# Sharing out the filling products of an attention pipeline: even fifths in the first fifteen slots

## The chip, the cores and the metric

The kernel runs on one core of one Trainium2 chip. The metric is the device time of one execution in microseconds (us). All numbers of the profile come from one profiled execution; times "at 46.00" are microseconds from the start of its span.

## The reference

One transformer block over 2048 tokens of width 512, in float32:

```
mod = silu(c) @ w_mod  -> sa, ca, ga, sb, cb, gb
h   = layernorm(x) * (1 + ca) + sa
x1  = x + ga * (attention(h) @ wo)
h2  = layernorm(x1) * (1 + cb) + sb
out = x1 + gb * (((h2 @ w_gate) * (h2 @ w_up)) @ w_down)      # F = 1376

attention: 32 heads of 16, in 4 segments of 512 tokens, per segment s and head:
  a_dot = softmax(q k^T / 4 + causal mask) v
  a_mem = (phi(q) M) / (phi(q) z + 1e-6)       # phi(t) = t+1 if t>0 else exp(t)
  o     = sigmoid(beta) * a_mem + (1 - sigmoid(beta)) * a_dot
  M += phi(k)^T v ;  z += sum phi(k)           # after the segment
```

## The kernel before

**Stages.** After a start of about 28 us (weights, the first layernorm, the first projections) comes the attention loop, and from about 500 us on the feed-forward part (lines from 1289 on). The change lies in the attention loop, in its first fifteen slots.

**The attention loop.** Work is cut into 32 units `u`; a unit is four heads of one segment, two units make one of the four head groups `g` of a segment. The loop over `v` from -2 to 32 is a software pipeline, and each `v` has five slots. In a slot stand, in the order in which the code is written:

- `q_half(u, i, 0)`: the products q_i_0 of the unit that is ahead (line 282). TensorE writes logits into PSUM bank `lq0`; VectorE reads them in a masked row-maximum scan (line 39, `CUSTOM_DVE_ANT_0`) that ends in a `DVE_READ_ACCUMULATOR2_ANT` and so frees the bank.
- `fill(share[slot], slot < 4)`: the filling products, see below.
- `q_half(u, i, 1)`: the same for bank `lq1` (q_i_1).
- `k_step(v, slot)`, for v from 0 on: the transposed logits of the unit in work, into the double bank `lk`; ScalarE takes the exponential (line 335, tile `pt`) and GpSimd zeroes the masked triangles (line 341, `AFFINE_SELECT`).

For v from 1 on, slot 1 also has the 32 products of `av_step` (tile `tb`).

**The filling products.** Two generators, `fa` and `fb`, hand out everything else that TensorE has to do meanwhile: the projections of the next head group and segment (vps, kps, qps: bank tiles of 12 products, handed out three at a time), the memory term (mp, mz) and others. Each call of `fill` adds `share * rate` to a credit, and takes pieces until the credit is used up:

```
def fill(share, mem):
    credit[0] += share * rate[0]          # rate[0] is 5.5 in every slot
    if mem:
        credit[0] -= mem_step() or 0.0    # mp: 0.5, mz: 0.9
    while credit[0] > 0:
        ...                               # w = next piece's weight
        credit[0] -= w                    # 0.68 for three products
```

When the twelve products of a projection are through, its pieces for the other engines follow (`a_kq`, line 800): ScalarE copies it (line 820, `qf`), casts it to bfloat16 (824), GpSimd subtracts (825, `qr`), ScalarE casts the rest (828), GpSimd subtracts again (829), and a transfer stores it (830, `qd`). `load(u)` brings stored q and k back as `qst` and `kst`.

**The next segment's layernorm** (`ln`, line 172) is woven into the same stream: VectorE takes statistics (`ast`, `amv`) of four tiles x_0 to x_3, ScalarE takes Ln and Exp (`asd` line 186, `ay` line 188), GpSimd refines the result in five small steps (lines 192, 196 to 199; the last writes `ay`), and VectorE scales x_0 to x_3 by `ay` (`TENSOR_SCALAR`).

**What sets the order.** TensorE's order is that in which the code is written (every product is tied to the one before). VectorE's is too, from this loop on (`vec.eng = CV`, a chain). The orders of ScalarE, GpSimd and of the transfers issued by SyncE are set by a list scheduler when the kernel is built; on the chip each engine keeps the order that it was given.

Of the kernel before, what the change touches and what calls it, by code (L numbers as in the profile page):

```python
# [57 lines left out]
def tile_kernel(ctx, tc, x, wq, wk_, wv, wo, beta, w_gate, w_up, w_down, c, w_mod, out):  # L58
# [58 lines left out]
    def flush():  # L117

        while later:
            later.pop(0)()  # L120

    def rest_of():

        while soon:
            soon.pop(0)()
# [116 lines left out]
    def run(gen):  # L242
        try:
            while True:
                next(gen)
        except StopIteration as e:
            return e.value
# [34 lines left out]
    def q_half(u, i, b):  # L282

        Q, K = qst[u % NB], kst[u % NB]
        if i == b == 0:
            nms[u] = ap.tile([P, 16], F32, tag="nm", name=f"nm{u}", bufs=2)
        nm = nms[u]
        h = i // 2 * 2 + b
        if i == 4:
            parts = ((2 * b, 1), (2 * b + 1, 1))  # L290
        else:
            parts = ((h, 3),) if i % 2 == 0 else ((h, 2), (h, 0))
        qp = psp.tile([P, L], F32, tag=f"lq{b}", name=f"q{u}_{i}_{b}", bufs=1)
        c = 0
        for hh, qb in parts:
            n = (qb + 1) * P
            MM(qp[:, c:c + n], Q[0:96, hh, qb * P:(qb + 1) * P], K[0:96, hh, 0:n], start=True, stop=True)
            c += n
        c = 0
        for hh, qb in parts:  # L300
            n = (qb + 1) * P
            vec.tensor_tensor_reduce(qp[:, c:c + n], qp[:, c:c + n], cmask[:, L - n:], -1.0, -NEG,
                                     ALU.add, ALU.min, nm[:, 4 * hh + qb:4 * hh + qb + 1])
            c += n

    def n_step(u):

        Q = qst[u % NB]
        tp = pst([16, P], "tb", f"ntp{u}")
        TP(tp, nms.pop(u), ident)  # L310
        nt = ap.tile([16, 2, P], BF, tag="nt", name=f"nt{u}", bufs=2)
        vec.tensor_copy(nt[:, 0], tp)
        vec.tensor_sub(nt[:, 1], tp, nt[:, 0])
        for i in range(2):
            lastnt[0] = nc.sync.dma_start(Q[96 + i:97 + i].rearrange("p h (q t) -> p (h q) t", t=P), nt[:, i])
# [29 lines left out]
    def av_step(u, kb):  # L345

        s, g, jq = u // 8, u // 2 % 4, u % 2
        if kb == 0:
            tbs[u] = pst([P, L], "tb", f"tb{u}", F32)
        n = L - kb * P  # L350
        for j in range(HQ):
            p, b = j // 2, j % 2
            hh = g * HG + jq * HQ + j
            if kb == 0:
                rhs, w = ptiles[u, p][:, b, :], sels[u, 1]
            elif kb == 2:
                rhs, w = ptiles[u, 4][:, p, 256 * b:256 * b + 256], sels[u, 4]
            else:
                c = 0 if kb == 1 else 384
                rhs, w = ptiles[u, 2 + p][:, b, c:c + n], sels[u, 3]  # L360
            x = MM(tbs[u][32 * j:32 * j + 32, kb * P:], vt[s % 2][kb][:, hh * VS:hh * VS + 32], rhs,
                   start=kb == 0, stop=kb == 2, tile_position=(0, 32 * j), skip_group_check=True)
            if j == 0:
                tc.add_manual_dep(x.ins, w.ins.name, SYNC, reason="all four heads")
        if kb == 2:
            tsbs[u] = ap.tile([P, L], F32, tag="tsb", name=f"tsb{u}", bufs=2)
            act.activation(tsbs[u], tbs.pop(u), AF.Copy)  # L367
# [140 lines left out]
    def wo_load(s, pool):  # L508
        rw = []
        for t in range(4):  # L510
            a = pool.tile([P, D], F32, tag="orl", name=f"orl{s}_{t}", bufs=4)
            n = D - P if s == NSEG - 1 else D
            pin(nc.sync.dma_start(a[:, 0:n], od[s][t][:, 0:n]))
            rw.append(a)
        return rw

    def wo_op(s, rw, us, gs=range(NG), stop=False):

        for g in gs:
            op = bank(f"op{s}_{g}", small=not stop)  # L520
            for t in range(4):
                a = rw[t][:, g * P:(g + 1) * P]
                if s == NSEG - 1 and g == NG - 1:
                    a = orows[NSEG * NG - 1][:, t].rearrange("p h e -> p (h e)")
                TP(op[:, t * P:(t + 1) * P], a, ident)
            nm = ("k", "q")[g % 2]
            i = s % 2 * 2 + g // 2
            oH = pw.tile([P, L], F32R, tag=f"w{nm}H{i}", name=f"oH{s}_{g}", bufs=1)
            oL = pw.tile([P, L], F32R, tag=f"w{nm}L{i}", name=f"oL{s}_{g}", bufs=1)
            ahead.append(act.activation(oH, op, AF.Copy))  # L530
            us.append((oH, oL))
            if stop:
                yield 0.45
                pin(vec.tensor_sub(oL, op, oH.bitcast(F32)))
            else:
                (soon if (s, g) in ((1, 0), (2, 1)) else later).append(lambda oL=oL, op=op, oH=oH: pin(vec.tensor_sub(oL, op, oH.bitcast(F32))))
                yield 0.45
            if stop and g % 2 == 1:
                yield False

    def xr_load(s, pool, tag="xr"):
        xrs = []
        for t in range(4):
            xr = pool.tile([P, D], F32, tag=tag, name=f"xr{s}_{t}", bufs=4)
            pin(nc.sync.dma_start(xr, x[rows(s, t), :]))
            xrs.append(xr)
        return xrs
# [530 lines left out]
    def fill(share, mem):  # L1078

        credit[0] += share * rate[0]  # L1080
        if mem:
            credit[0] -= mem_step() or 0.0
        while credit[0] > 0:
            for f in (fa, fb):
                try:
                    w = next(f)
                    break
                except StopIteration:
                    w = None
            if w is False:  # L1090
                return
            if w is None:
                credit[0] = min(credit[0], 0.5)
                return
            credit[0] -= w

    def until(*key):
        while key not in done:
            credit[0] -= (mem_step() if len(key) == 3 and memq else next(fa)) or 0.0
# [50 lines left out]
    load(1)  # L1150
    btag[:] = ["ms"]
    vec.eng = CV
    share = (0.25, 0.0, 0.25, 0.25, 0.25)
    for v in range(-2, NQ + 1):
        rate[0] = 5.5
        on, prev = 0 <= v < NQ, 0 <= v - 1 < NQ
        for slot in range(5):
            i = (slot + 3) % 5
            u = v + 2 if i < 3 else v + 1
            if 0 <= u < NQ:  # L1160
                q_half(u, i, 0)
            flush()
            if prev and slot == 1:
                for kb in (0, 1, 3, 2):
                    av_step(v - 1, kb)
            if v == NQ and slot == 0:
                assert B["orl_free"]
                o3 = wo_load(3, wpool)
                xr3 = xr_load(3, B["pb"])
            if v == NQ and slot == 2:  # L1170
                for f in (fa, fb):
                    for _ in f:
                        pass
                btag[:] = ["lq0", "lq1", "ms"]
                us3 = []
                run(wo_op(3, o3, us3, range(NG - 1), True))
                lg1 = lnC(1, wpool, lambda: pc, wpool, "orl", 4, lambda name: dbank(name))
                next(lg1)
            if prev and slot == 4:
                if (v - 1) % 2 == 0 and v > 8:  # L1180
                    until((v - 1) // 8, (v - 1) // 2 % 4, 0)
                t_step(v - 1)
                if (v - 1) % 8 == 7:
                    osegs[0] += 1
            if slot == 2 and prev and (v - 1) % 8 == 7:
                vfree[0] = (v - 1) // 8 + 2
            fill(share[slot], slot < 4)
            rest_of()
            if 0 <= u < NQ:
                q_half(u, i, 1)  # L1190
            if on:
                k_step(v, slot)
            while after:
                after.pop(0)()
            while behind:
                behind.pop(0)()
            if slot == 2 and 0 <= v + 1 < NQ:
                n_step(v + 1)
                if v + 3 < NQ:
                    load(v + 3)  # L1200
            if slot == 1 and 3 <= v + 3 < NQ:
                until((v + 3) // 8, (v + 3) // 2 % 4)
# [95 lines left out]
    def dbank(name):  # L1298
        nd[0] += 1
        return pst((P, 512), ("lq0", "lk0", "lq1", "lk1")[nd[0] % 4], name)  # L1300
# [381 lines left out]
```

## Time and profile before

| | |
|---|---|
| three runs | 853.47, 853.55, 854.69 us; median 853.55 |
| the profiled execution | 854.15 us, span 852.4 us |
| TensorE busy | 835.3 us, 98% |
| VectorE busy | 643.1 us, 75% |
| ScalarE busy | 499.0 us, 59% |
| GpSimd busy | 276.8 us, 32% |
| granted TensorE clock | 1.000 |

In the profile PE is TensorE's products, DVE VectorE, ACT ScalarE, POOL GpSimd, SPq the transfers that SyncE issues. A row of the timeline has start, duration, engine, source line, operation, tiles (output<-input, numbers left out), shapes and a count where several are merged; in brackets stands the idle time of the engine just before the row and who ended it. The end of a product is modelled: products that follow each other overlap in the rows, and the distance of their starts tells how fast they are issued.

### The profile page before, as it was taken

The page shows a single profiled execution, that of the slowest core. Times are in us where ns is not written, and L with a number is a line of the kernel's source. Part 1 is how long each engine was busy: PE and PEld are TensorE (multiplying, and loading weights), DVE is VectorE, ACT ScalarE, POOL GpSimd, SP SyncE. Part 2 cuts the span into 40 slices and gives each one's busy share as a digit, 9 for nine tenths or more (in the row PEclk, how much of TensorE's full clock was granted, in tenths as well). Part 3 has the DMA queues.
Part 4 walks back from the last instruction along what each step waited for, and adds up shares of the span by engine and source line. Part 5 has one row for each costly group of instructions (what it writes and reads, how often), then busy time and mean ns, then how long its engine had stood idle before and what let it go on. Part 6 is the DMA issues. An engine that isn't in the chain of part 4 may idle for free.

```text
span 852.4 us, 14404 instructions
## 1 busy us (share of the span) xinstructions
PE 835.3 (98%) x4972; PEld 597.4 (70%) x4972; DVE 643.1 (75%) x1797; ACT 499.0 (59%) x760; POOL 276.8 (32%) x423
## 2 busy tenths in 40 slices
PE   9989999999999999999999999999999999999998
PEld 6756656666665656666665687888888778888886
DVE  7897768887778967787888359989987855447654
ACT  4758767787676876677545626344435555555330
POOL 2756627566565774675434610000000000000000
PEclk9999999999999999999999999999999999999999
DMA  9645435563545554466675466587650685335102
GB/s 271 155 152 155 121 104 141 158 179 115 143 106 166 144 165 106 122 170 213 195 216 155 145 192 230 189 287 271 253 201 28 234 271 210 121 135 184 43 8 98
DMA packets 83928, 139.57 MB, mean 164 GB/s; under 512 B 12720, under 2 KB 46768, under 8 KB 83856
## 3 DMA queue, kind: packets, MB, share of 16 engines
q1 hardware_dynamic: 83424, 138.51, 52.0%
q8 instruction: 39, 0.64, 0.3%
q14 instruction: 33, 0.27, 0.1%
q10 hardware_dynamic: 432, 0.15, 0.1%
HBM read 89.87 MB, written 48.50 MB: 162 GB/s over the span
## 4 chain that ended last, share of the span: by engine, by line
PE 61%; DVE 5%; ACT 1%; issue 0%; POOL 0%; DVEq 0%
PE acc L1358 14%; PE Xg L1289 7%; PE Xu L1289 6%; PE wops L85 5%; PE tb L85 5%; PE Yu L1289 4%; PE Yg L1289 4%; PE k L85 3%; PE q L85 3%; DVE q L39 2%; PE Zg L1289 1%; PE Zu L1289 1%; PE qps L85 1%; PE vps L85 1%; PE Xx L1289 1%; PE up L85 1%
## 5 line engine op out<-in xcount | busy, mean ns | idle before, releaser
L39 DVE CUSTOM_DVE_ANT_0 q<-q,cmask 128x384 f32<-128x384 f32 (+3 forms) x512 | 248.2, 503 | 71.1 <-PE q L85 63.5
L335 ACT ACTIVATE pt<-k 128x1024 f32<-128x1024 f32 x160 | 164.0, 1025 | 74.2 <-PE k L85 71.4
L341 POOL TENSOR_SCALAR_AFFINE_SELECT pt<-pt 128x256 f32<-128x256 f32 (+1 forms) x224 | 98.0, 452 | 137.2 <-ACT pt L335 136.9
L85 PE MATMUL q<-kst,qst 96*128 96x384 bf16 (+3 forms) x512 | 122.8, 302 | 6.5 <-DVE nm L39 5.1
L85 PE MATMUL k<-qst,kst 98*128 98x384 bf16 (+3 forms) x512 | 96.0, 299 | 1.6 <-ACT pt L335 1.3
L1366 DVE TENSOR_TENSOR xa<-xa,acc 128x512 f32<-128x512 f32 x95 | 64.9, 684 | 39.6 <-PE acc L1358 37.8
L85 PEld LDWEIGHTS <-qst 96*128 96x128 bf16 x512 | 43.9, 98 | 58.4 <-issue 43.6
L85 PE MATMUL tb<-pt,v 128*32 128x512 f32 (+3 forms) x1024 | 75.5, 436 | 0.0
L39 DVE DVE_READ_ACCUMULATOR2_ANT nm<- 128x1 f32 x512 | 71.8, 140 | 0.0
L85 PEld LDWEIGHTS <-kst 98*128 98x128 bf16 x512 | 44.4, 98 | 24.9 <-issue 8.8
L1358 PE MATMUL acc<-dH,mH 128*128 128x512 f32 (+1 forms) x152 | 60.3, 397 | 0.0
L1358 PE MATMUL acc<-dL,mH 128*128 128x512 f32 (+1 forms) x152 | 60.1, 395 | 0.0
L1358 PE MATMUL acc<-dH,mL 128*128 128x512 f32 (+1 forms) x152 | 60.0, 395 | 0.0
L85 PEld LDWEIGHTS tb<-pt,v 128*32 128x32 f32 x1024 | 28.7, 109 | 38.6 <-issue 35.7
L367 ACT ACTIVATE tsb<-tb 128x512 f32<-128x512 f32 x32 | 19.1, 596 | 31.6 <-PE tb L85 31.5
L1358 PEld LDWEIGHTS acc<-dH,mL 128*128 128x128 f32 (+1 forms) x152 | 28.5, 188 | 7.1 <-DVE mL L1309 0.3
L1358 PEld LDWEIGHTS acc<-dL,mH 128*128 128x128 f32 (+1 forms) x152 | 28.6, 188 | 7.0
L1358 PEld LDWEIGHTS acc<-dH,mH 128*128 128x128 f32 (+1 forms) x152 | 28.5, 188 | 6.8
L85 PE MATMUL kps<-ahH,wkH 128*128 128x512 f32 x64 | 29.4, 460 | 0.0
L85 PE MATMUL qps<-ahH,wqH 128*128 128x512 f32 x64 | 28.7, 448 | 0.2 <-DVE oL L39 0.2
L85 PE MATMUL vps<-wvH,ahH 128*128 128x512 f32 x64 | 28.3, 442 | 0.0
L85 PE MATMUL wops<-woH,oH 128*128 128x512 f32 x64 | 28.3, 442 | 0.0
(403 smaller groups left out, 2019.1 us busy)
## 6 DMA issues: line engine op xcount, KB each, us to landing
wm<-in_w_mod_dram SPq DMA_DIRECT2D x24, 256.0 KB, 3.9
kd<-k SPq DMA_DIRECT2D x16, 384.0 KB, 2.5
qd<-q SPq DMA_DIRECT2D x16, 384.0 KB, 3.5
kst<-kd SPq DMA_DIRECT2D x32, 192.0 KB, 3.2
qst<-qd SPq DMA_DIRECT2D x32, 192.0 KB, 3.7
x<-in_x_dram SPq DMA_DIRECT2D x16, 256.0 KB, 4.8
kst<-kd SPq DMA_DIRECT2D x32, 128.0 KB, 3.2
qst<-qd SPq DMA_DIRECT2D x32, 128.0 KB, 3.7
```

The lines of the kernel that those rows point to most:

```text
L39: i = getattr(self.eng, name)(*a, **k)
L85: return pe(nc.tensor.matmul(*a, **k))
L335: ex = act.activation(pt, kp, AF.Exp, scale=0.25)
L341: sels[u, i] = nc.gpsimd.affine_select(w, w, pattern=[[0, w.shape[1]], [1, P]], compare_op=ALU.is_ge, fill=0.0, base=0, channel_multiplier=-1)
L367: act.activation(tsbs[u], tbs.pop(u), AF.Copy)
L1289: pe(nc.tensor.matmul(ps[0:n], a, b[:, k], start=first and c == 0, stop=last and c == 5, skip_group_check=True))
L1358: pe(nc.tensor.matmul(ps, a[0:m, t * P:(t + 1) * P], b[0:m], start=j == 0, stop=j == n - 1))
L1366: vec.tensor_add(xa, xa, ps)
```

## The change

The shares of a slot are chosen anew for every `v`. As long as no unit is through (`prev` is false: v = -2, -1 and 0, fifteen slots), each of the five slots gets a fifth; afterwards the old shares hold. The credit of one `v` is 5.5 in both.

```
-    share = (0.25, 0.0, 0.25, 0.25, 0.25)
     for v in range(-2, NQ + 1):
         rate[0] = 5.5
         on, prev = 0 <= v < NQ, 0 <= v - 1 < NQ
+        share = (0.25, 0.0, 0.25, 0.25, 0.25) if prev else (0.2,) * 5
         for slot in range(5):
             i = (slot + 3) % 5
```

Pieces are taken whole, so most stay in their slot. Three groups of three products move on TensorE. The last three of vps_2 come ahead of the first scan product of unit 0 (q_0_0) instead of behind it. The three of kps_2 that use ahH_2 and ahL_2 come behind q_3_1, q_4_0 and the transposes mp_0 of unit 0 instead of ahead of them. The last three of qps_2 move furthest.

This is TensorE at the end of the second `v` and the start of the third; q_ are scan products of unit 1, k_0 the first transposed logits of unit 0, qps_2 the q projection of head group 2. Before:

```order
L88 MATMUL mp_1_768<-ident,phk_1_539 128x128 x4
L85 MATMUL qps_2_732<-ahH_3_397,wqH_517 128x512
L85 MATMUL qps_2_732<-ahH_3_397,wqL_518 128x512
L85 MATMUL qps_2_732<-ahL_3_398,wqH_517 128x512
L85 LDWEIGHTS qst_187
L85 MATMUL q_3_1_787<-kst_183,qst_187 128x384
L85 LDWEIGHTS qst_187
L85 MATMUL q_3_1_787<-kst_183,qst_187 128x128
L85 LDWEIGHTS kst_182
L85 MATMUL k_0_792<-qst_186,kst_182 128x512
L85 LDWEIGHTS kst_182
L85 MATMUL k_0_792<-qst_186,kst_182 128x512
```

The same place now, from the second product of k_0 on:

```order
L85 MATMUL k_0_780<-qst_186,kst_182 128x512
L85 LDWEIGHTS qst_187
L85 MATMUL q_4_0_786<-kst_183,qst_187 128x256
L85 LDWEIGHTS qst_187
L85 MATMUL q_4_0_786<-kst_183,qst_187 128x256
L85 MATMUL mz_1_791<-v_0_162,pkr_1_773 128x136
L85 MATMUL mz_1_791<-v_1_163,pkr_1_773 128x136
L85 MATMUL mz_1_791<-v_2_164,pkr_1_773 128x136
L85 MATMUL mz_1_791<-v_3_165,pkr_1_773 128x136
L85 MATMUL qps_2_732<-ahH_3_397,wqH_517 128x512
L85 MATMUL qps_2_732<-ahH_3_397,wqL_518 128x512
L85 MATMUL qps_2_732<-ahL_3_398,wqH_517 128x512
```

The last three products of qps_2 stood between mp_1 and q_3_1; now they stand behind mz_1, directly ahead of q_4_1.

What hangs on qps_2 moves with it on the other engines. On GpSimd the place is the stretch from the subtraction of the k projection of group 2 to the layernorm's last step; qr_2 (line 825) and q_0_2 (line 829) belong to qps_2, ayb and aya and ay to the layernorm, pt_0 to pt_3 are the masks of unit 0. Before:

```order
L825 TENSOR_TENSOR qr_2_784<-qf_2_781,q_0_2_783 128x512
L341 AFFINE_SELECT pt_0_795<-pt_0_795 128x2x128
L829 TENSOR_TENSOR q_0_2_783<-qr_2_784,q_0_2_783 128x512
L341 AFFINE_SELECT pt_1_817<-pt_1_817 128x2x128
L196 TENSOR_SCALAR ayb_869<-amv_746 128x4
L341 AFFINE_SELECT pt_2_842<-pt_2_842 128x2x128 x2
L192 TENSOR_TENSOR aya_868<-ay_866 128x4
L197 TENSOR_TENSOR ayb_869<-ayb_869,aya_868 128x4
L198 TENSOR_SCALAR ayb_869<-ayb_869 128x4
L199 TENSOR_TENSOR ay_866<-ay_866,ayb_869 128x4
L341 AFFINE_SELECT pt_3_892<-pt_3_892 128x2x128 x2
```

The same stretch now:

```order
L341 AFFINE_SELECT pt_0_783<-pt_0_783 128x2x128
L341 AFFINE_SELECT pt_1_817<-pt_1_817 128x2x128
L825 TENSOR_TENSOR qr_2_806<-qf_2_803,q_0_2_805 128x512
L196 TENSOR_SCALAR ayb_869<-amv_746 128x4
L341 AFFINE_SELECT pt_2_842<-pt_2_842 128x2x128 x2
L829 TENSOR_TENSOR q_0_2_805<-qr_2_806,q_0_2_805 128x512
L192 TENSOR_TENSOR aya_868<-ay_866 128x4
L197 TENSOR_TENSOR ayb_869<-ayb_869,aya_868 128x4
L341 AFFINE_SELECT pt_3_892<-pt_3_892 128x2x128
L198 TENSOR_SCALAR ayb_869<-ayb_869 128x4
L341 AFFINE_SELECT pt_3_892<-pt_3_892 128x2x128
L199 TENSOR_TENSOR ay_866<-ay_866,ayb_869 128x4
```

The subtraction of line 829 now stands just ahead of the layernorm's aya, and the two masks of pt_3, which followed the layernorm's last step, now stand among its steps. On ScalarE pt_0 now precedes the copy of qps_2, and that projection's casts stand behind pt_1 and behind asd. On VectorE only the statistics of x_2 move: from ahead of q_3_1's scan of unit 1 to behind the mz_1 step, ahead of q_4_1's scan. Among the transfers the store of that q projection moves behind the first piece of the load for unit 3. From v = 1 on all engines have their old order, apart from the k projection of group 3, whose last cast and subtraction go ahead of pt_4's exponential and mask.

More of the change, by code (lines that the diff above doesn't have):

```diff
@@ L1152, in tile_kernel @@
     vec.eng = CV
-    share = (0.25, 0.0, 0.25, 0.25, 0.25)
     for v in range(-2, NQ + 1):
@@ L1156, in tile_kernel @@
         on, prev = 0 <= v < NQ, 0 <= v - 1 < NQ
+        share = (0.25, 0.0, 0.25, 0.25, 0.25) if prev else (0.2,) * 5
         for slot in range(5):
```

## The prediction

> **What bounds the kernel now.** First the page's busy times, then the waits, then stretches around the fifteen slots (they run from about 35 to 67).
>
> ```profile
> PE 835.3 (98%) x4972; PEld 597.4 (70%) x4972; DVE 643.1 (75%) x1797; ACT 499.0 (59%) x760; POOL 276.8 (32%) x423
> PE q L85 <- DVE nm L39: 5.1, 11, 1.0
> DVE x L39 <- POOL ay L199: 0.4, 1, 0.4
> 54.00:57.00 3.00, 1.98 (x15) 1.45 (x14) 2.90 (x13) 2.26 (x4) 2.62 (x4) 1.00 0.43 134
> 67.00:70.00 3.00, 3.00 (x39) 1.60 (x39) 2.86 (x10) 2.41 (x4) 1.52 (x2) 1.00 0.04 10
> ```
>
> PE is busy for 98% of the span, so a microsecond that PE stands still anywhere is a microsecond at the end, unless PE waits less later. Its largest wait is for DVE: a scan product needs its bank freed by the last read of the scan before. The two stretches (length, then PE, PEld, DVE, ACT, POOL, clock, DMA) show two regimes. At 54 to 57 DVE is busy for 2.90 of 3.00 us and PE only for 1.98: the scans pace everything. At 67 to 70 PE is full. So the change is judged by what it does to DVE's chain of scans up to about 67, and after that by how late PE is. DVE waits only once in the kernel for the layernorm's `ay`, for 0.4 us; that wait will matter most.
>
> **The first move** (vps_2 ahead of q_0_0 of unit 0).
>
> ```profile
> 33.57 3.80 DVE L853 SCALAR_TENSOR_TENSOR phk<-phk,rlk 128x512 f32<-128x512 f32 x1 [1.02 <-ACT phk L848]
> 36.81 0.39 PE L85 MATMUL vps<-wvH,ahH 128*128 128x512 f32 x1
> ```
>
> Products start 0.23 apart, so q_0_0 moves to just ahead of 36.81, at about 36.6. DVE is busy with the phk step until 37.37 and a scan can begin 0.43 after its product (the next rows: 43.59 and 44.02), 37.03. Cost nothing, covered by 0.3 us.
>
> **The second move** (three products of kps_2 behind q_3_1, q_4_0 and mp_0).
>
> ```profile
> 43.59 0.61 PE L85 MATMUL q<-kst,qst 96*128 96x384 bf16 x4
> 44.02 0.57 DVE L39 CUSTOM_DVE_ANT_0 q<-q,cmask 128x384 f32<-128x384 f32 x1 [0.31 <-PE q L85]
> 45.09 0.38 PE L85 MATMUL q<-kst,qst 96*128 96x256 bf16 x2 [0.45 <-DVE nm L39]
> 45.81 0.14 DVE L39 DVE_READ_ACCUMULATOR2_ANT nm<- 128x1 f32 x1
> 46.00 0.38 PE L85 MATMUL q<-kst,qst 96*128 96x512 bf16 x1 [0.53 <-DMA qd<-q]
> ```
>
> DVE waited 0.31 us for q_3_1 at 44.02. That product now comes 3 x 0.23 = 0.7 us sooner, and the wait is gone. PE loses nothing: the 0.45 us that it idled ahead of q_4_1 now lie ahead of q_4_0, and the three products fill the later gap. Does the gain survive 46.00? The row blames a transfer, but DVE's read ends at 45.95, 0.05 us earlier, the distance that the other bank waits show (below: 55.01 to 55.06), so I read it as a bank wait that moves along. The three products now also delay q_4_1's release, which may eat the gain. Bounds 0 and -0.31; I take the middle, **-0.15 us**.
>
> **The third move** (three of qps_2 behind k_0, q_4_0, mz_1). PE first.
>
> ```profile
> 54.87 0.14 DVE L39 DVE_READ_ACCUMULATOR2_ANT nm<- 128x1 f32 x1
> 55.06 0.38 PE L85 MATMUL q<-kst,qst 96*128 96x256 bf16 x2 [0.66 <-DVE nm L39]
> 55.28 1.09 PE L85 MATMUL mz<-v,pkr 128*128 128x136 f32 x8
> 56.73 0.38 PE L85 MATMUL q<-kst,qst 96*128 96x256 bf16 x2 [0.36 <-DVE nm L39]
> 56.95 0.59 PE L85 MATMUL k<-qst,kst 98*128 98x512 bf16 x2
> 58.32 0.40 PE L85 MATMUL kps<-ahL,wkH 128*128 128x512 f32 x1
> 58.52 0.14 DVE L39 DVE_READ_ACCUMULATOR2_ANT nm<- 128x1 f32 x1
> 58.71 0.38 PE L85 MATMUL q<-kst,qst 96*128 96x512 bf16 x1
> 84.46 1.09 PE L85 MATMUL mz<-v,pkr 128*128 128x136 f32 x8
> 86.09 0.39 PE L85 MATMUL q<-kst,qst 96*128 96x512 bf16 x1
> ```
>
> q_4_0 stays at 55.06: its bank is freed by the read that ends at 54.87 + 0.14 = 55.01. Then mz and three products take 86.09 - 84.46 = 1.63 us (the same two steps, later in the trace), so q_4_1 starts at 55.28 + 1.63 = 56.91 instead of 56.73: 0.18 late. DVE does not feel it, with its scans queued one behind the other, and PE loses it again at q_0_1: the products end their issue at 58.32 + 0.23 = 58.55, and the bank comes free at 58.66, so q_0_1 stays at 58.71. Cost 0 on PE. The statistics of x_2 change places inside a full DVE stretch; before q_4_1's scan the sum of work is the same: 0.
>
> Now what hangs on qps_2. ACT and POOL:
>
> ```profile
> 54.13 0.63 ACT L824 ACTIVATE q<-qf 128x512 bf16<-128x512 f32 x1
> 55.06 1.15 POOL L825 TENSOR_TENSOR qr<-qf,q 128x512 f32<-128x512 f32 x1
> 56.94 1.16 POOL L829 TENSOR_TENSOR q<-qr,q 128x512 bf16<-128x512 f32 x1 [0.38 <-ACT q L828]
> 57.58 1.03 ACT L335 ACTIVATE pt<-k 128x1024 f32<-128x1024 f32 x1 [0.72 <-PE k L85]
> 61.40 0.20 POOL L192 TENSOR_TENSOR aya<-ay 128x4 f32<-128x4 f32 x1
> 61.95 0.14 DVE L39 DVE_READ_ACCUMULATOR2_ANT nm<- 128x1 f32 x1
> 62.03 1.03 ACT L335 ACTIVATE pt<-k 128x1024 f32<-128x1024 f32 x1 [1.02 <-PE k L85]
> 62.25 0.20 POOL L199 TENSOR_TENSOR ay<-ay,ayb 128x4 f32<-128x4 f32 x1
> 62.48 0.55 DVE L39 TENSOR_SCALAR x<-x,amv,ay 128x512 f32<-128x512 f32 x1 [0.40 <-POOL ay L199]
> 63.13 0.77 POOL L341 TENSOR_SCALAR_AFFINE_SELECT pt<-pt 128x256 f32<-128x256 f32 x2 [0.68 <-ACT pt L335]
> 63.51 0.40 PE L85 MATMUL qps<-ahL,wqH 128*128 128x512 f32 x1
> 63.81 0.14 DVE L39 DVE_READ_ACCUMULATOR2_ANT nm<- 128x1 f32 x1
> 64.01 0.38 PE L85 MATMUL q<-kst,qst 96*128 96x512 bf16 x1
> ```
>
> Before, POOL ran its small steps from 61.40 on, 0.28 apart, wrote `ay` at 62.25, and only then waited for pt_3 (ACT until 63.06, masks from 63.13, two in 0.77, so 0.39 each). Now the masks stand among the small steps. From 63.13: mask 0.39, step 198 0.28, mask 0.39, so `ay` starts at 64.19, ends 0.20 later, and DVE's scaling of x_0 starts 0.03 behind that (62.45 to 62.48): **64.42 instead of 62.48, 1.94 late**.
>
> The second path to the same step is the moved subtraction. k_1 starts at 57.13, its exponential 0.63 later (56.95 to 57.58), at 57.76; then the cast of line 824 at about 58.7 (0.63), qr_2 from 59.4 (1.15), the second cast from 60.8 (0.6, by the row of the first), line 829 from 61.5 (1.16), and aya at 62.6, ayb at 62.9. The first mask waits until 63.13 anyway: both paths end within 0.05 us of each other, so 1.94 doesn't hang on one of them.
>
> Who waits: DVE is in order, so behind x_0's scaling the scan of q_1_1 is queued, and behind its bank PE's q_2_1 (scan's last read ends at 63.95, product at 64.01). PE has six products to issue meanwhile, through at 63.51 + 0.23 = 63.74; before, it was 0.27 us early, now it stands from 63.74 to 65.95. The scans that follow are spaced as before, and after the 32 products of tb PE is full (the stretch at 67), with nothing to catch up from.
>
> ACT's copies stay ahead of their users: pt_0 comes sooner, pt_4 now waits for k's last cast, but with the products 1.9 us late it has that time. The transfers: q's store now stands behind one piece of unit 3's load, and waits for line 829's end at about 62.7.
>
> ```profile
> 64.03 1.76 SPq L274 DMA_DIRECT2D qst<-qd  x3
> 70.98 0.38 PE L85 MATMUL q<-kst,qst 96*128 96x512 bf16 x1
> ```
>
> The load's last pieces were issued from 64.03 on; the store is out by then, and unit 3's first product came only at 70.98. Cost nothing, 5 us of cover behind the last issue.
>
> **The sum.** 0 + 0 - 0.15 + 1.94 = +1.8 us; with all of the early gain +1.63, with none +1.94. The profiled execution was 854.15 (852.4 of span and 1.75 around it), 0.60 over the median of the runs; on the median 853.55 this gives **855.4 us**, between 855.2 and 855.5 for this case. What a measurement of this kernel can tell from no change is about 0.2%, 1.71 us, here 855.26: the case lies mostly, not wholly, on the slower side.
>
> **The rivals.**
>
> *The loss is caught up (not slower).* The delay enters DVE and PE at 64, but if PE idles later for causes that do not move along, it shrinks. For it: ACT's and DMA's chains were not all late. Against it: PE's 98%, and 3.00 of 3.00 right behind. It decides once 0.7 us of later idle time gives way, out of PE's largest class of waits of 5.1 us in all, part of which lies behind this place; up to 1.7 us are conceivable. A loss of 0.1 to 1.1 us remains: 853.65 to 854.65, 13%.
>
> *The masks don't hold the layernorm's step back.* If pt_3 were ready much sooner, only the early gain would be left: 853.3 to 853.55, 5%. Against it: pt_3's products follow k_2 and a full ACT chain.
>
> *DVE loses to POOL as well.* The phk step took 3.80 us at 33.57 while POOL was subtracting, against 0.69 in the following row.
>
> ```profile
> 33.54 1.69 POOL L765 TENSOR_TENSOR wkL<-wrk,wkH 128x512 fp32r<-128x512 f32 x1
> 66.95 0.69 DVE L39 SCALAR_TENSOR_TENSOR phk<-phk,rlk 128x512 f32<-128x512 f32 x1 [0.38 <-ACT phk L848]
> 68.00 1.16 POOL L829 TENSOR_TENSOR k<-kr,k 128x512 bf16<-128x512 f32 x1 [1.38 <-ACT k L828]
> ```
>
> POOL began 0.03 ahead and DVE paid 3.1. At 66.95 the order was DVE first, POOL's subtraction at 68.00; now that subtraction and pt_4's mask stand ahead of the phk step in time, by about 0.4 us. If they slip into it, DVE loses 0.6 to 1.2 more: 856.0 to 856.6, 14%. The Trainium skill, SBUF — State Buffer, "Who interferes with whom", gives the rule: a VectorE operation with two SBUF inputs and a GpSimd one that reads SBUF share a port pair, and whichever starts first holds it. The trace agrees at 33.57.
>
> *Faster.* The scans could run closer from 43 to 57, where PE idles 0.45, 0.53, 0.66 and 0.36 us; all of it gone is 2.0 us, 851.6. Against it: DVE's 2.90 of 3.00. 8%.
>
> **How the numbers follow.** The forecast case has 60%. Of its interval from 1.63 to 1.94 a quarter lies below 1.71: 45% slower, 15% same. Slower 45 + 14 = 59%; same 15 + 13 + 5 = 33%; faster 8%. The range reaches down to the lower end of the caught-up case, 853.6, and up to the top of the port case and 0.4 us more, a third of the spread between the three runs (1.22 us), 857.0. Outside are faster, the bare gain and a few per cent above.
>
> **What would show it.** Right: DVE's wait for `ay` grows from 0.4 to about 2.3 us, x_0's scaling starts at about 64.3, PE idles about 2 us ahead of q_2_1, and everything from 67 on is the same trace about 1.8 later. Wrong: x_0's scaling before 63.5, or PE's total idle time unchanged. The early gain shows as a scan of q_3_1 at 43.6 to 43.7.

## The result, and the profile after

The changed kernel takes 856.93 us (median of five runs, 856.33 to 858.67) against 853.59: **3.34 us slower**, ratio 1.0039, 95% interval 1.0028 to 1.0050. Forecast were 855.4 and a range from 853.6 to 857.0: the sign and the range hold, but the loss is nearly twice the +1.8 of the sum. The profiled execution took 856.93 us too, span 855.2.

First the waits of the changed kernel (total us, times, longest):

```profile
PE q L85 <- DVE nm L39: 7.6, 12, 1.9
DVE x L39 <- POOL ay L199: 2.2, 1, 2.2
```

DVE's wait for `ay` grew from 0.4 to 2.2 us, PE's waits for scan banks from 5.1 to 7.6. The timeline of DVE at the places of which the prediction spoke:

```profile
43.65 0.60 DVE L39 CUSTOM_DVE_ANT_0 q<-q,cmask 128x384 f32<-128x384 f32 x1
54.66 0.14 DVE L39 DVE_READ_ACCUMULATOR2_ANT nm<- 128x1 f32 x1
64.08 0.55 DVE L39 TENSOR_SCALAR x<-x,amv,ay 128x512 f32<-128x512 f32 x1 [2.16 <-POOL ay L199]
```

The early gain is there: q_3_1's scan starts at 43.65 instead of 44.02, and of that 0.21 us are left at the read that frees q_4_0's bank (54.66, before 54.87). Then x_0's scaling starts at 64.08 instead of 62.48, 1.60 late. The timeline of GpSimd ahead of it:

```profile
61.40 1.15 POOL L829 TENSOR_TENSOR q<-qr,q 128x512 bf16<-128x512 f32 x1
62.52 0.20 POOL L192 TENSOR_TENSOR aya<-ay 128x4 f32<-128x4 f32 x1
62.95 0.41 POOL L341 TENSOR_SCALAR_AFFINE_SELECT pt<-pt 128x256 f32<-128x256 f32 x1
63.33 0.19 POOL L198 TENSOR_SCALAR ayb<-ayb 128x4 f32<-128x4 f32 x1
63.47 0.41 POOL L341 TENSOR_SCALAR_AFFINE_SELECT pt<-pt 128x256 f32<-128x256 f32 x1
63.84 0.20 POOL L199 TENSOR_TENSOR ay<-ay,ayb 128x4 f32<-128x4 f32 x1
```

The moved subtraction of line 829 runs at 61.40, where aya ran before, and the two masks stand among the small steps; `ay` starts at 63.84 instead of 62.25. So far everything goes as forecast. Now TensorE:

```profile
53.38 0.38 PE L85 MATMUL q<-kst,qst 96*128 96x384 bf16 x2 [1.17 <-DVE nm L39]
54.85 0.38 PE L85 MATMUL q<-kst,qst 96*128 96x256 bf16 x2 [0.66 <-DVE nm L39]
65.60 0.38 PE L85 MATMUL q<-kst,qst 96*128 96x512 bf16 x1 [1.85 <-DVE nm L39]
67.96 0.63 PE L85 MATMUL qps<-ahH,wqL 128*128 128x512 f32 x1
68.39 0.63 PE L85 MATMUL qps<-ahL,wqH 128*128 128x512 f32 x1
69.90 0.38 PE L85 MATMUL q<-kst,qst 96*128 96x256 bf16 x2
```

PE stands 1.85 us ahead of q_2_1 (65.60 instead of 64.01, 1.59 late). But at 67.96 its products start 0.43 apart, not 0.23, and q_4_0 of the next round comes at 69.90, in the kernel before at 66.69: 3.21 late. The loss doubles within four microseconds behind the standstill, where PE is never idle. Three stretches of the changed kernel, each 3.41 us long (length, then PE, PEld, DVE, ACT, POOL busy, granted clock, DMA share, GB/s):

```profile
52.60:56.01 3.41, 1.97 (x15) 1.49 (x15) 3.34 (x14) 1.77 (x3) 1.87 (x2) 1.00 0.47 126
62.84:66.25 3.41, 1.55 (x9) 0.96 (x9) 2.14 (x8) 1.85 (x4) 2.42 (x6) 1.00 0.89 233
66.25:69.66 3.41, 3.41 (x14) 2.21 (x12) 2.96 (x10) 2.58 (x5) 1.86 (x2) 0.50 0.74 226
```

**From 66.25 to 69.66 the granted clock is 0.50.** The 3.41 us ahead of it hold the standstill, and PE was busy in them for 1.55 us, 45%. A fall to half for 3.41 us costs half of that, 1.7 us, if PE is full; here 3.21 - 1.59 = 1.62. In the kernel before, the poorest stretch of this length from 36 to 73 us is the first of these two, with 2.12; the second is the counterpart of the one with the standstill:

```profile
53.20:56.61 3.41, 2.12 (x14) 1.46 (x14) 3.31 (x14) 2.81 (x5) 2.89 (x3) 1.00 0.52 142
62.80:66.21 3.41, 3.31 (x21) 2.24 (x20) 3.35 (x12) 2.84 (x5) 2.39 (x4) 1.00 0.75 202
```

Its clock never fell there. The mean clock over a whole execution shows such a fall without a trace of it: one makes 1 - 0.5 x 3.41/855 = 0.998, two make 0.996. All five runs of the changed kernel have 0.995 to 0.998. Of 81 runs of the kernel before, made beside the experiments, none is below 0.999.

### The profile page after: what moved, and what is told of

Read it like the earlier page. It is cut to its first block, busy times and chain, and to the rows that moved or that the text cites. A ratio compares the mean times of both kernels' runs of the same rounds, so it can differ in the third digit from the quotient of the medians.

```text
span 855.2 us, 14405 instructions
## 1 busy us (share of the span) xinstructions
PE 835.1 (98%) x4972; PEld 598.0 (70%) x4972; DVE 643.4 (75%) x1797; ACT 498.7 (58%) x760; POOL 276.0 (32%) x423
## 4 chain that ended last, share of the span: by engine, by line
PE 59%; DVE 6%; ACT 2%; issue 1%; DMA 0%; POOL 0%; SPq 0%; DVEq 0%; ACTq 0%
PE acc L1358 14%; PE Xg L1289 6%; PE Xu L1289 6%; PE wops L85 5%; PE tb L85 5%; PE Yu L1289 4%; PE Yg L1289 4%; PE k L85 3%; PE q L85 3%; DVE q L39 2%; PE Zg L1289 1%; PE Zu L1289 1%; PE qps L85 1%; PE vps L85 1%; PE Xx L1289 1%
```

## The experiments

Theory: the late `ay` costs 1.6 us as forecast, and the rest is the clock. Rival: the rest is another delay behind the standstill, in which the low clock only accompanies it. In what follows "fell" means a mean clock of 0.998 or less in a run. Results come beside runs of the kernel before on the same chip: 853.77 us (27 runs) for the first four, 853.68 (28) for the next four, 853.69 (11) and 853.64 (15) for the last two pairs.

**e1: work for TensorE in the standstill.** The changed kernel with nine products into an unused bank ahead of q_2_1.

```
+            if v == 0 and slot == 4:          # ahead of q_half(u, i, 1)
+                dps = pst((P, 512), "sm", "dps")
+                for _ in range(9):
+                    MM(dps, kst[0][0:96, 0, 0:P], kst[0][0:96, 0, :], start=True, stop=True)
```

> The changed kernel with nine more 96x128 by 512 products on TensorE (0.22 us each, into a bank that nobody reads) put where it stands still, ahead of q_2_1. Theory (late ay stalls PE, and the standstill lowers the clock): the wait of VectorE for ay stays at 2.2 us and q_2_1 stays at 65.6, but the granted clock stays at 1.00, products at 67 are 0.23 us apart again, and the time is 1.6 us below the changed kernel: 855.0 to 855.5. Rival (the clock falls for the lull at 52 to 57, or for a cause outside this stretch): clock still 0.5 for 3 us, 856.5 to 857.

Measured: 857.15 us, ratio 1.0033 [1.0021, 1.0046]. The profiled execution took 855.58 with a clock of 1.00, but three of six runs fell (857.71 to 858.01); the three others have a median of 855.84. So filling the standstill doesn't suffice: there is a second place. Of the profiled execution, the poorest stretch:

```profile
51.80:55.21 3.41, 1.57 (x12) 0.91 (x11) 3.34 (x11) 2.02 (x3) 1.47 (x1) 1.00 0.71 150
```

It is the place from which the change took the last three products of qps_2: PE now waits 1.17 and 0.66 us there for scan banks (53.38 and 54.85 above), where it waited 0.43 and 0.66 before. The first of these waits in the kernel before:

```profile
53.59 0.38 PE L85 MATMUL q<-kst,qst 96*128 96x384 bf16 x2 [0.43 <-DVE nm L39]
```

**e2: the layernorm's refinement left out.** The changed kernel without the five GpSimd steps for segment 1; `ay` keeps the value that ScalarE gave it.

```
+        if not (pfx == "a" and s == 1):
             eng.tensor_mul(a, y, y)
...
             eng.tensor_mul(y, y, b)
```

> The changed kernel without GpSimd's five small steps in the layernorm of segment 1 (the refinement of ay is left out; VectorE takes ScalarE's value). TensorE's and VectorE's orders are those of the changed kernel. Theory: the scaling of x_0 starts at about 61.8 to 62.0, PE doesn't stand still at 63.6, the clock stays at 1.00, and only the early gain is left: 853.0 to 853.5. Rival (the moved products themselves cost): the loss stays in large part, 855 to 857.

Measured: 853.36 us, ratio 0.9996 [0.9985, 1.0008]. x_0 no longer waits:

```profile
60.95 1.16 POOL L830 TENSOR_TENSOR q<-qr,q 128x512 bf16<-128x512 f32 x1
61.50 0.89 DVE L39 TENSOR_SCALAR x<-x,amv,ay 128x512 f32<-128x512 f32 x1
```

The scaling takes 0.89 us here instead of 0.55, beside the subtraction that is still running (line 829, 830 in this kernel). Two of ten runs fell (855.79, 855.98), though the standstill is gone: the early place alone can do it.

**e3: the fifths in the first ten slots alone.**

```
-        share = (0.25, 0.0, 0.25, 0.25, 0.25) if prev else (0.2,) * 5
+        share = (0.25, 0.0, 0.25, 0.25, 0.25) if v >= 0 else (0.2,) * 5
```

> The kernel before with fifths in the first ten slots only (v = -2 and -1): the first two moves without the third. Theory: the scan of q_3_1 starts at 43.65, everything up to 61 is 0.2 to 0.3 us sooner, GpSimd's order is that of before and so is the wait of 0.4 us for ay: 853.2 to 853.5. Rival (the early gain is lost at a transfer at 46.00): 853.5 to 853.7, nothing moved at 62.

Measured: 853.46 us, ratio 0.9999 [0.9990, 1.0009], no run of ten fell. No variant of the change is faster than the kernel before by an amount that can be measured (e2 has 0.9996, this one 0.9999). The first two moves bring x_0 0.30 us forward, and its wait for `ay` stays:

```profile
62.18 0.55 DVE L39 TENSOR_SCALAR x<-x,amv,ay 128x512 f32<-128x512 f32 x1 [0.38 <-POOL ay L199]
```

**e4: the fifths in the third v alone**, the condition `if v != 0` in the same line.

> The kernel before with fifths in the slots of v = 0 only: the third move alone. Theory: ay late by 1.9 us against before, PE standing still for about 2.2 us, clock down: 857.0 to 857.5, a little above the changed kernel because the early gain is missing. Rival (the three moves add up, or the clock falls only with the lull at 53 that the earlier moves help to make): 855 to 856.

Measured: 856.36 us, ratio 1.0029 [1.0016, 1.0041]; four of ten runs fell, the six others have a median of 855.27 (854.98 to 856.72). The whole loss comes from the third move. The profiled execution, 859.62 us, fell twice; the stretches ahead of each fall and the falls:

```profile
51.83:55.24 3.41, 1.61 (x12) 0.96 (x11) 3.34 (x12) 2.11 (x3) 1.42 (x1) 1.00 0.66 149
55.24:58.65 3.41, 3.41 (x14) 2.64 (x14) 2.39 (x11) 0.41 (x2) 0.41 (x1) 0.50 0.34 115
65.48:68.89 3.41, 0.82 (x7) 0.58 (x7) 3.14 (x8) 0.72 (x2) 2.48 (x4) 1.00 0.87 248
68.89:72.31 3.42, 3.42 (x13) 2.19 (x12) 3.01 (x10) 2.54 (x4) 0.63 (x1) 0.50 0.44 140
```

The falls begin 13.65 us apart, four times 3.41: as if the clock were decided on a grid of stretches of 3.41 us.

**e5: work at the early place alone.** The changed kernel with six products ahead of q_3_1 of unit 1 and three ahead of q_4_0.

```
+    def busy(*at):
+        tag, n = {(0, 0, 1): ('tb', 6), (0, 1, 0): ('tb', 3)}.get(at, ("", 0))
+        if n:
+            dps = pst((P, 512), tag, "dps")
+            for _ in range(n):
+                MM(dps, kst[0][0:96, 0, 0:P], kst[0][0:96, 0, :], start=True, stop=True)
...
+            busy(v, slot, 0)                  # ahead of q_half(u, i, 0)
...
+            busy(v, slot, 1)                  # ahead of q_half(u, i, 1)
```

> The changed kernel with nine more products on TensorE in the lull at 52 to 55 (six ahead of q_3_1 of unit 1, three ahead of q_4_0; 0.22 us each, bank tb), none in the standstill at 63.6. Theory A (the standstill at 63.6 alone lowers the clock): the lower clock at 66 to 70 stays in nearly every run, median about 856.9. Theory B (what counts is all the idle time of the last 10 us or so, so that the lull at 52 to 57 shares in it): falls become rarer, some runs at 855.0 to 855.5 with clock 1.000, median 855.5 to 856.5.

Measured: 855.76 us, ratio 1.0029 [1.0017, 1.0040]; two of seven runs fell (857.37, 857.56), the others have 855.70. The late place alone can do it as well.

**e6: both places filled**, the table of e5 with `(0, 4, 1): ('sm', 9)` added.

> Both sets of additional products: nine in the lull at 52 to 55 and nine in the standstill at 63.6. The wait for ay stays (2.2 us, scaling of x_0 at 64.1). Either theory of the clock: no fall in any run, clock 0.999 to 1.000 throughout, median 855.2 (855.0 to 855.6), so that what is left of the loss is VectorE's wait alone, +1.5. Rival (the clock falls for something else): half of the runs still at 857 to 858, as with nine products in the standstill alone.

Measured: 855.31 us (ten runs from 854.94 to 855.70), ratio 1.0017 [1.0008, 1.0027], **none fell**. Of the profiled execution x_0's scaling, and the poorest stretch:

```profile
63.87 0.55 DVE L39 TENSOR_SCALAR x<-x,amv,ay 128x512 f32<-128x512 f32 x1 [2.15 <-POOL ay L199]
42.10:45.51 3.41, 2.89 (x19) 1.86 (x18) 3.27 (x15) 1.02 (x2) 0.24 (x1) 1.00 0.99 312
```

The wait for `ay` stays, and with the clock held the loss is +1.63: about the forecast term, alone. The extra products lie in time in which PE waited; against the 855.10 of the changed kernel's one run without a fall (e9) they show no cost clear of the spread of the runs. The rival falls: x_0 is 1.39 late here, and only 0.24 us are left beside that when the clock stays up.

**e7: the masks of pt_3 behind `ay`.** The changed kernel with one order added for GpSimd; `aylast[0]` holds the layernorm's last step.

```
+            if (u, i) == (0, 3):
+                tc.add_manual_dep(sels[u, i].ins, aylast[0].ins.name, NOSYNC, reason="order")
```

> The changed kernel with the two masks of pt_3 tied behind the layernorm's last small step on GpSimd, as they stood before; line 829 of the q projection stays ahead of the steps. Theory (GpSimd's order is the cause): the steps run at 62.5, 62.8, 63.1, 63.35, the scaling of x_0 starts at 63.6 instead of 64.1, VectorE's wait is 1.7 instead of 2.2 us; runs without a fall of the clock at 854.6. Rival (the masks only fill waiting time): x_0 stays at 64.1.

Measured: 854.84 us, ratio 1.0019 [1.0009, 1.0028]; three of ten runs fell, the others have 854.70, 1.0 us above the kernel before.

```profile
63.56 0.60 DVE L39 TENSOR_SCALAR x<-x,amv,ay 128x512 f32<-128x512 f32 x1 [1.68 <-POOL ay L201]
65.13 0.38 PE L85 MATMUL q<-kst,qst 96*128 96x512 bf16 x1 [1.43 <-DVE nm L39]
```

Without the masks in between, x_0 comes 0.52 us sooner than in the changed kernel and is still 1.08 late: that much is the subtraction of line 829 alone, the prediction's second path. So the prediction's "1.94 doesn't hang on one of them" is right in part: a third of the delay goes with the masks. No run has the masks without the subtraction. They wait for pt_3's exponential, which in the changed kernel waited for TensorE's product and ends at 61.85 + 1.03 = 62.88; by this row, an estimate, the masks alone would make the whole 1.60.

```profile
61.85 1.03 ACT L335 ACTIVATE pt<-k 128x1024 f32<-128x1024 f32 x1 [0.64 <-PE k L85]
```

**e8: the late `ay` alone, in the kernel before.** Four more small GpSimd steps (each multiplies `ay` by 1), and the old shares.

```
+        if pfx == "a" and s == 1:
+            for _ in range(4):
+                eng.tensor_scalar(y, y, 1.0, 0.0, op0=ALU.mult, op1=ALU.add)
```

> The kernel before (old shares) with four more small steps on GpSimd ahead of aya in the layernorm of segment 1 (each multiplies ay by 1): 61.40 + 4 x 0.28, the pt_3 masks come in behind, ay at 64.05, the scaling of x_0 at 64.3, 1.8 us late, with TensorE's and VectorE's orders of before. Theory: the same standstill ahead of q_2_1, so +1.8 us in runs without a fall (855.4) and 857 or more with one; the loss of the changed kernel is had without moving one product. Rival (the moved products are needed for the loss): under 854.5.

Measured: 855.62 us, ratio 1.0023 [1.0014, 1.0032]; two of ten runs fell (856.32, 856.98), the others have 855.48.

```profile
64.37 0.55 DVE L39 TENSOR_SCALAR x<-x,amv,ay 128x512 f32<-128x512 f32 x1 [2.09 <-POOL ay L202]
65.90 0.38 PE L85 MATMUL q<-kst,qst 96*128 96x512 bf16 x1 [1.78 <-DVE nm L39]
62.80:66.21 3.41, 1.63 (x8) 1.03 (x7) 1.80 (x6) 1.91 (x4) 2.52 (x7) 1.00 0.74 177
```

x_0 is 1.89 late and the time without falls 1.80 longer: no product was moved, so the delay needs nothing else of the change.

**e9: the changed kernel once more**, unaltered, to see how often it falls.

> The changed kernel again, for how often the clock falls. Theory (two idle stretches, at 52 to 57 and at 63.6, each lowering the clock in some executions and not in others): runs with clock 0.999 to 1.000 at 855.0 to 855.5, runs with 0.998 or less at 856.3 to 858.7, both kinds present; five of five low in the first measurement was chance, median 855.5 to 856.9. Rival (the fall is certain in this kernel): all runs at 0.998 or less, median 856.9.

Measured: 857.76 us (855.10 to 859.59), ratio 1.0047 [1.0033, 1.0061]; five of six runs fell, with the first five 10 of 11. The one without took 855.10. The profiled execution, 858.64 us, fell twice:

```profile
50.98:54.39 3.41, 1.58 (x11) 0.87 (x10) 3.31 (x12) 1.71 (x3) 1.42 (x1) 1.00 0.80 193
54.39:57.80 3.41, 3.39 (x13) 2.79 (x12) 2.60 (x10) 0.42 (x1) 0.46 (x2) 0.50 0.34 117
64.63:68.04 3.41, 0.38 (x3) 0.25 (x3) 2.75 (x6) 1.16 (x2) 2.65 (x5) 1.00 0.87 247
68.04:71.45 3.41, 3.41 (x15) 2.30 (x14) 2.73 (x10) 2.55 (x4) 0.87 (x2) 0.50 0.59 173
```

Again 13.65 us lie between the falls. The second standstill is longer here, for a reason that the timeline shows:

```profile
65.25 1.15 POOL L825 TENSOR_TENSOR kr<-kf,k 128x512 f32<-128x512 f32 x1
65.25 1.43 DVE L39 TENSOR_SCALAR x<-x,amv,ay 128x512 f32<-128x512 f32 x1 [2.51 <-POOL ay L199]
```

After an early fall x_0's scaling meets a GpSimd subtraction that starts with it, and takes 1.43 us instead of 0.55 (in e4's profiled execution 1.38). After an early fall the late stretch is thus poorer still: 0.38 us of work here, against 1.55 without one.

**e10: a longer delay in the kernel before**, e8 with seven steps.

> The kernel before with seven more small steps on GpSimd ahead of aya; the masks of pt_3 and the subtraction of line 825 of k_3 come in between, so ay is written at about 66.1 and the scaling of x_0 starts at about 66.4, 3.9 us late; PE stands still for about 4.1 us ahead of q_2_1. Theory (the longer the standstill, the surer the fall): the clock falls in nearly every run, 0.998 or less, and the time is 853.7 + 3.9 + 1.5 to 3 = 859.1 to 860.6. Rival (chance of a fall doesn't depend on the length): most runs at 0.999 to 1.000 and 857.6.

Measured: 858.76 us (857.30 to 859.76), ratio 1.0056 [1.0042, 1.0071]; three of four runs fell. PE's product, and stretches:

```profile
67.26 0.59 PE L85 MATMUL q<-kst,qst 96*128 96x512 bf16 x1 [3.59 <-DVE nm L39]
62.73:66.14 3.41, 0.94 (x5) 0.51 (x4) 0.41 (x1) 1.84 (x4) 2.73 (x8) 1.00 0.85 207
66.14:69.55 3.41, 2.29 (x10) 1.60 (x10) 3.14 (x11) 0.87 (x2) 1.15 (x1) 0.50 0.47 141
69.55:72.97 3.42, 3.42 (x16) 1.68 (x18) 2.64 (x10) 2.10 (x5) 0.64 (x1) 0.50 0.01 3
```

The low clock lasts 6.83 us here, twice 3.41, although PE is back at work at 67.26: it comes back at an end of the grid, and the 2.29 us of work in the first stretch did not suffice for that.

**e11 and e12: where the bound lies.** By now six falls were profiled. PE was busy for 0.38 to 1.62 us in the 3.41 us ahead of each, and for 1.97 or more in those stretches of the same four executions at full clock that led to none. e11 adds three products at each place, e12 one: the table of e5 with `(0, 0, 1): ('tb', 3), (0, 4, 1): ('sm', 3)`, and with 1 for each 3.

> The changed kernel with only three extra products in each of the two idle places (six and three at the first, nine at the second, had removed every fall). Theory, from the profiles so far: the clock is decided on a fixed grid of 3.41 us, and falls to half for the next stretch when TensorE was busy for less than about half of one (at most 1.62 of 3.41 us ahead of the six falls seen, at least 1.98 in stretches that did not lead to one). Three products add about 0.7 us to the poorest 3.41 us of each place: 1.58 becomes about 2.25, above the bound and above the 2.12 of the kernel before. Expected: no fall in about ten executions (mean clock never below 0.999), 855.3 us, although TensorE still stands for about 0.5 us at the first place and for about 1.2 us ahead of q_2_1. Rival, any standstill of over a microsecond may bring a fall: 3 or more of ten executions at 0.998 or below, 855.5 to 857.5.

Measured: 855.62 us, ratio 1.0021 [1.0012, 1.0031]; **none of nine runs fell**. PE still stands, but the poorest stretches are above 2.2:

```profile
65.38 0.38 PE L85 MATMUL q<-kst,qst 96*128 96x512 bf16 x1 [1.20 <-DVE nm L39]
51.80:55.21 3.41, 2.23 (x15) 1.21 (x14) 3.31 (x12) 2.13 (x3) 1.58 (x2) 1.00 0.61 143
62.80:66.21 3.41, 2.21 (x14) 1.15 (x13) 2.32 (x8) 1.84 (x3) 2.30 (x6) 1.00 0.80 242
```

> The same with one extra product at each place: the poorest 3.41 us have about 1.8 us of busy TensorE, between the 1.62 that brought a fall and the 1.98 that didn't. If the bound is above 1.8, falls stay about as frequent as in the changed kernel (about 7 of 10 executions or more at 0.998 or below, 856.5 to 857.5 us); if it is below 1.8, there are none and the time is 855.3. Either way x_0 starts at about 64.0.

Measured: 859.65 us (855.13 to 860.80), ratio 1.0051 [1.0032, 1.0070]; four of six runs fell, all four twice by their clock (0.995 and 0.996). Times beyond 859 had not been expected; an early fall brings the late one here. The profiled execution:

```profile
51.77:55.18 3.41, 1.78 (x12) 1.02 (x11) 3.31 (x12) 2.12 (x3) 1.64 (x2) 1.00 0.70 143
55.18:58.59 3.41, 3.41 (x13) 2.29 (x12) 2.61 (x11) 0.60 (x1) 0.23 (x1) 0.50 0.33 115
```

A stretch with 1.78 us of work, 52%, still leads to a fall. That is no sharp bound, though. An execution that kept its clock shows its grid too, since the clock falls once more when the work is over. In the changed kernel this last fall is at 854.73, 785.07 us or 230 times 3.4133 behind 69.66, so the grid runs on unbroken. In e5's profiled execution it is at 853.93; 232 lengths earlier, at 62.04, a stretch begins that holds the standstill:

```profile
62.04:65.45 3.41, 1.74 (x7) 1.19 (x7) 1.31 (x6) 2.09 (x3) 2.95 (x8) 1.00 0.65 188
65.45:68.86 3.41, 3.23 (x24) 2.08 (x27) 3.00 (x12) 3.00 (x5) 2.05 (x3) 1.00 0.71 188
853.50:853.92 0.42, 0.00 (x0) 0.00 (x0) 0.00 (x0) 0.00 (x0) 0.00 (x0) 1.00 0.00 0
853.93:854.30 0.37, 0.00 (x0) 0.00 (x0) 0.00 (x0) 0.00 (x0) 0.00 (x0) 0.50 0.00 0
```

It has 1.74 us of work, and the clock stays up. Over all profiled executions, stretches of the grid at full clock with up to 1.62 us led to a fall and those with 1.80 or more did not; in between, 1.78 fell, 1.74 and 1.68 (the last work of the kernel before, from 847.00) did not. The bound is at about half of 3.41 us, and these records, whose ends of products are modelled, give it no closer. The longest pause doesn't decide: PE stood for 1.67 us without a break in this stretch of e5 (from 63.78 on), and for 1.13 us at most in the one ahead of e4's first fall.

## Why the prediction was right or wrong

*The first move, cost nothing; the second, -0.15.* Right: e3, which has both alone, is no slower than before, and x_0 comes 0.30 us forward. The gain at 54.87 is 0.21 us, between the middle and the upper bound; a total time doesn't resolve it.

*The third move on GpSimd, +1.94 at x_0.* The mechanism is right, the size a little high: x_0 came at 64.08, 1.60 late, where the sum with its gain had 64.27. The second path was as estimated (aya at 62.52, estimate 62.6). On the first, the mask ran at 62.95 instead of 63.13, since the early gain reaches pt_3 as well, and the steps around the masks stand 0.14 apart (63.33 to 63.47), not 0.28: together the 0.34 us by which the sum without the gain, 64.42, is too late. e2 takes the loss away, e8 makes it without the change, and with the clock held e6 leaves +1.63 against the sum's +1.8. Over the kernels, the time of runs that didn't fall follows x_0's start in the profiled execution to within 0.6 us:

| kernel | x_0 against before's 62.48 | time against before, runs that didn't fall |
|---|---|---|
| e2 | -0.98 | -0.53 |
| e3 | -0.30 | -0.31 |
| e7 | +1.08 | +1.0 |
| e11 | +1.38 | +1.98 |
| e6 | +1.39 | +1.63 |
| e5 | +1.62 | +2.02 |
| e1 | +1.67 | +2.07 |
| e8 | +1.89 | +1.80 |

*"Nothing to catch up from" behind it.* Right within a fraction: in the profiled execution the delay is 3.21 at 69.90 and 2.8 in the span, so 0.4 are given back. The rival that the loss is caught up didn't happen.

*Where it failed: the third move's "cost 0 on PE", and the standstill "from 63.74 to 65.95".* Both were priced by their length alone. That taking three products out of the lull at 52 to 55 loses no time is right, and so is the length of the standstill (to 65.60). But each thins a stretch of 3.41 us below what the clock needs, from 2.12 and 3.31 us of busy PE to about 1.6 in both. The term that the sum lacks is a fall in most runs, at one place or at both. It cost 1.62 us in the profiled execution, and from 1.2 us (e8) to 2.6 (e2) between the medians of one kernel's runs with one fall and without. The executions of the changed kernel that didn't fall, or had it prevented, took 855.10, 855.31 (e6) and 855.62 (e11): the forecast 855.4. "Everything from 67 on is the same trace about 1.8 later" is the sentence that the profile refutes.

*The range held partly by luck.* It reaches up to 857.0 for the rival in which DVE loses to POOL, not for the clock, and that rival didn't happen in the form it was given. The measured 856.93 is just inside; the same kernel measured again, 857.76 (e9), is not.

*DVE loses to POOL.* Not at the phk step where I looked for it: it takes 0.69 us in the changed kernel as before. But a scaling of x_0 slowed beside a subtraction appeared, 0.89 us instead of 0.55 in e2 and 1.35 to 1.43 us after an early fall (e4, e9, e12). The 3.1 us that the prediction put down to the subtraction at 33.54 aren't the price of one: a second one follows on it, from 35.17 for 1.65 us. The Trainium skill, SBUF — State Buffer, "Who interferes with whom", says that a scaling of one tensor may take the shared port pair too; the 1.43 us beside a subtraction that starts at the same 65.25 agree.

*The clock.* The Trainium skill, TensorE: Matmul & The Clock Gate, "What's actually happening", describes a gate with two states, half and full, decided over windows of about 3.4 us that run freely. The traces agree: 0.50 and 1.00, falls of 3.41 and 6.83 us, and 13.65 between two in one execution (e4, e9). The rule that the page gives under "HAM oscillation", no idle gaps over about 3.4 us, would have predicted no fall, and here the measurement decides: standstills of 1.85 us, and waits of 1.17 and 0.66 with work between, sufficed. e11, e12 and e5's stretch beside e4's show that what counts is the work in a window.

*Which executions fall.* A fall comes when a stretch of the grid happens to lie on a thin place. Read back from the last fall, the grid's position differs among the 14 profiled executions, spread over 3.0 of the 3.41 us. That accounts for those which kept their clock: the stretches of the grid at the early place hold 2.17 us of work in e1 (from 52.87) and 2.16 in e2 (from 50.57), although sliding ones with 1.57 and 1.58 lie close by. So whether one execution falls is luck, and so are the five of five of the first measurement.

*What stays open.* With a bound of 1.78 us, starts within about 1.2 of 3.41 us are thin at the early place and within about 2.1 at the late one, which would make falls in 3 and in 6 of 10 runs if the grid lay at random. With the early place alone open 8 of 26 runs fell (e1, e2, e7), which fits; with the late one alone 4 of 17 (e5, e8), where 10 would be expected. The count hangs on the bound: with 1.62 us, e8 has no thin start at all. But one of e10's four runs kept its clock where every position of the grid should have found a thin window by either bound. It is also open why a fall costs 2.2 and 2.6 us in e1 and e2, more than half of 3.41, and why some runs without a fall took over 856 us: 856.02 and 856.72 in e4, 856.59 in e1, 856.21 in e8, 856.46 in e11, and 856.40 once in the kernel before.

## What to carry to other kernels

Read the busy time of TensorE in sliding stretches of 3.4 us, not only its waits: where it drops to about half (falls came here after up to 52%) the clock may halve for the next stretch. An idle time that cost nothing by itself then cost 1.2 to 2.6 us here. The mean granted clock of every run tells it (0.998 is one such fall in 855 us), and three short products in each of the two waits held the clock (e11), at no cost clear of the spread of the runs. When products move, follow what their results feed on an in-order engine: here a subtraction and two masks ahead of a step of 0.2 us made VectorE and TensorE 1.6 us late.

## What the hardware showed that had not been expected

- The clock fell after a 3.41 us window that was still 52% busy (e12, 1.78 us), not only after an idle one; another with 1.74 us kept it (e5), so half is as close as these records come to a bound.
- It stayed at half for one window of 3.41 us where that window was full of work, and for two, 6.83 us, where the first held only 2.29 us (e10).
- The windows run on unbroken through an execution, and their position differed among the 14 profiled ones, spread over 3.0 of 3.41 us.
- A VectorE scaling of one 128x512 tensor took 1.43 us instead of 0.55 beside a GpSimd subtraction that started at the same moment.
